# Another order for the first half of a hand-ordered attention and gated-MLP kernel

## The chip, the cores and the metric

The kernel runs on one core of a Trainium2 chip. The time is device time in microseconds; the span is the part of it that one profiled execution covers, from the first instruction's start to the last one's end. The core's engines work side by side, each through its own list of instructions in order: PE multiplies (PEld is its loading of weights), DVE, ACT and POOL work on tiles, and SP issues transfers between the chip's memory and the core's. Semaphores hold an instruction until what it needs is there.

## The reference

A retention layer without a softmax (8 batches, 8 heads, 576 positions, 64 numbers per head) makes x, and one gated MLP with a mixing over positions follows.

```python
scores = scale * np.matmul(q, k.transpose(0, 1, 3, 2))
Dmat = np.where(rel >= 0, gamma[:, None, None] ** rel[None, :, :], 0.0)
x = np.matmul(scores * Dmat, v)          # then heads side by side: (8, 576, 512)

h = gelu(x @ w_in)                       # w_in 512 x 1024, tanh form
u, v = (h[..., :512], h[..., 512:])
v_n = (v - mu) / np.sqrt(var + 1e-06) * g_ln
v_s = np.einsum('ts,bsd->btd', w_sg, v_n) + b_sg[None, :, None]
return (x + (u * v_s) @ w_out).astype(np.float32)
```

## The kernel before

**Tiling.** Two batches make a pair, and there are four pairs. A pair's 1152 rows are nine tiles of 128, so the output has 36 tiles, numbered 0 to 35. The attention is worked in blocks of one or two tiles, five per pair, so twenty blocks, 0 to 19 (of 2, 2, 1, 2 and 2 tiles). For a block, k, q and v are loaded (L457, or L460 in two halves for the one-tile blocks), scaled by powers of gamma and cast (L503; k at L493), q and k are turned by PE (L540) and copied out by DVE (L555), the scores (L591) are masked by DVE into `ret` (L604, L607), and the prefix product of k and v (L627) goes into a running sum (L652, L655), which lets a block do without the scores against all blocks ahead of it. The output (L673) is drained by ACT into `xT` (L730).

**The MLP.** Each tile of x is multiplied with the V half of w_in (L741); ACT applies the gelu (L748), DVE takes mean and variance (L756, L757), POOL the reciprocal root in four small operations (L761 to L764), and ACT writes the normalised tile (L776; L773 for the middle tile, which both batches of a pair share). The U half is multiplied at L788 and drained with a gelu at L798. When a batch's tiles are there, the mixing product with w_sg (L807) runs, DVE multiplies it with u (L817), and each output tile is a product with w_out and the addition of x (L833, L838). The first nine tiles are drained by ACT (L853), the later ones by DVE together with the addition of x (L855), for which SP turns x by a transfer (L847). SP stores each tile (L860).

**Things that happen once.** PE starts with "fillers", multiplications of zeros into a scratch tile that nothing reads (L357). The V half of w_in is loaded first (L381 into `xT`), the U half later (L381 into `uT`); DVE (L388) and ACT (L390) cast them. w_sg comes in three loads (L402 twice, L406), is cast by ACT into `wnat` (L413), turned by PE (L921) and copied by DVE (L925). The vectors g_ln and b_sg are turned by PE (L866) and worked into `col` by ten small DVE operations (L870 to L880), and PE turns them back into rows (L887, DVE L891). w_out is loaded into `uT` (L424).

**What sets the order.** Each of these steps is a job with a number, an engine, the jobs that it needs and the buffers that it takes. A string, `ORDER`, names the jobs in a row; a job's place among those of its own engine is its place in that engine's program, and `f10` in the string is a filler of ten units (two units make one multiplication of 128x256). The planner computes start times with its own costs only to bring the jobs of different engines into one sequence for the program; the order on each engine is that of the string. Buffers go round in rings (eight `ld`, three `vb`, four `ob`, two `pp` of PSUM), and a job that takes a buffer waits for the last reader of it. All loads, the turning transfers and all stores are issued by SP, one after another: an issue whose buffer is not free, or a store whose tile is not yet drained, holds what stands behind it.

Of the kernel before, what the change touches and what calls it, by code (L numbers as in the profile page):

```python
# [22 lines left out]
PR = dict(PB0=10000.0, O=4000.0, PB=9900.0, S=2000.0, S2=400.0, Z=1901.0, V=6000.0, V2=900.0, U=1260.0, W=4000.0, WS=19000.0, slack=60.0, pen=500.0)  # L23

ORDER = (
# [33 lines left out]
)  # L59


# [1144 lines left out]
```

## Time and profile before

| | |
|---|---|
| time, median of 3 runs | 214.62 us (214.43 to 214.93) |
| span of the profiled execution | 211.4 us |
| busy: PE, DVE, ACT, POOL | 197.6, 152.5, 116.8, 118.3 us |
| moved by transfers | 48.37 MB |

In the profile a row of a timeline gives the start and length of a group of instructions, its engine, line, operation and tiles, how many they are, and in brackets how long the engine stood idle before and what released it. The table by stretches gives busy times between two moments, the clock that PE was granted (1.00 is full), and the share of time in which the transfer engines had packets (it can pass 1, since packets overlap).

### The profile page before, as it was taken

Reading aid. Unit: us, or ns where it says so; the run is one execution under the profiler, and the core shown is the slowest. Engines: PE = TensorE matmul, PEld = TensorE weight load, DVE = VectorE, ACT = ScalarE, POOL = GpSimd, SP = SyncE. Lnnn points to the kernel's source line nnn. Section 1 sums busy time; section 2 is a strip of 40 time slices with the busy share of each in tenths; the row PEclk is TensorE's granted clock in tenths of the full one; section 3 lists DMA queues with packets and bytes.
Section 4 is the critical chain, followed back from the end, with each engine's and each line's share of the span. In section 5 each row is a group of like instructions: output and inputs, shape, how many; then the busy total and the mean of one; then the engine's idle time right before and its main releaser. Section 6 shows DMA issues by size and latency. Waiting matters only on the chain.

```text
span 211.4 us, 7911 instructions
## 1 busy us (share of the span) xinstructions
PE 197.6 (93%) x3384; PEld 137.8 (65%) x3416; DVE 152.5 (72%) x291; ACT 116.8 (55%) x207; POOL 118.3 (56%) x169
## 2 busy tenths in 40 slices
PE   7939999988999999999999999999999999999992
PEld 6727586666676677666767677566677675656661
DVE  3296498877888287967888875897865688576673
ACT  5230598892486954579585452776248349334400
POOL 8735158998667859993769679147582313022000
PEclk9985999999999999999999999999999999999999
DMA  6999999999899999999999999999999902586655
GB/s 164 335 276 305 170 374 295 231 291 340 192 248 296 296 324 276 214 328 189 243 285 109 243 307 206 198 323 182 222 172 148 270 0 78 149 153 174 176 172 198
DMA packets 85910, 48.37 MB, mean 229 GB/s; under 512 B 37035, under 2 KB 79283, under 8 KB 85875
## 3 DMA queue, kind: packets, MB, share of 16 engines
q1 hardware_dynamic: 85856, 47.87, 97.3%
q8 instruction: 26, 0.43, 0.9%
q14 instruction: 10, 0.07, 0.2%
q10 hardware_dynamic: 18, 0.00, 0.0%
HBM read 32.79 MB, written 9.44 MB: 200 GB/s over the span
## 4 chain that ended last, share of the span: by engine, by line
PE 79%; DVE 9%; issue 3%; POOL 3%; DMA 3%; ACT 1%; DVEq 0%; SPq 0%; POOLq 0%
PE wp L807 17%; PE hu L788 13%; PE op L838 13%; PE hv L741 12%; PE scr L357 6%; PE pp L673 6%; PE pp L591 4%; PE pp L540 3%; DMA ld<-in_v_dram 3%; DVE ret L604 2%; PE zp L627 2%; POOL vb L503 1%; DVE bst L756 1%; PE op L833 1%; POOL qb L503 1%
## 5 line engine op out<-in xcount | busy, mean ns | idle before, releaser
L807 PE MATMUL wp<-wT,vn 128*128 128x288 bf16 x256 | 41.1, 286 | 0.7 <-issue 0.6
L503 POOL TENSOR_TENSOR vb<-ld,gpow 128x1024 bf16<-128x1024 f32 (+1 forms) x20 | 34.5, 1731 | 11.6 <-DMA ld<-in_v_dram 8.8
L604 DVE TENSOR_TENSOR ret<-pp,msk 128x1024 bf16<-128x1024 f32 x32 | 38.3, 1215 | 3.4 <-PE pp L591 3.4
L788 PE MATMUL hu<-xT,w_in 128*128 128x256 bf16 (+1 forms) x320 | 36.8, 262 | 0.2
L817 DVE TENSOR_TENSOR uT<-wp,uT 128x288 bf16<-128x288 f32 x64 | 27.6, 451 | 12.4 <-PE wp L807 11.2
L741 PE MATMUL hv<-w_in,xT 128*128 128x512 bf16 x122 | 34.7, 380 | 1.7 <-ACT xT L730 0.3
L838 PE MATMUL op<-w_out,uT 128*128 128x512 bf16 (+1 forms) x138 | 34.4, 373 | 0.6 <-issue 0.2
L776 ACT ACTIVATE vn<-vg,mv 128x512 bf16<-128x512 f32 x32 | 25.3, 809 | 15.3 <-POOL mv L764 15.2
L748 ACT ACTIVATE vg<-hv 128x512 f32<-128x512 f32 x36 | 21.3, 596 | 21.8 <-PE hv L741 16.6
L788 PEld LDWEIGHTS <-w_in 128*128 128x128 bf16 x320 | 28.1, 98 | 7.2 <-issue 0.8
L756 DVE BATCH_NORM_STATS2 bst<-vg 128x6 f32<-128x512 f32 x36 | 24.7, 685 | 9.3 <-ACT vg L748 9.3
L730 ACT ACTIVATE xT<-pp 128x512 bf16<-128x512 f32 (+1 forms) x40 | 20.8, 550 | 18.1 <-PE pp L673 18.1
L807 PEld LDWEIGHTS <-vn 128*128 128x128 bf16 x256 | 24.4, 98 | 9.6 <-issue 0.7
L761 POOL TENSOR_SCALAR mv<-mv 128x2 f32<-128x2 f32 (+1 forms) x20 | 4.5, 224 | 44.7 <-DVE mv L757 37.8
L503 POOL TENSOR_TENSOR qb<-ldq,gpow 128x1024 bf16<-128x1024 f32 x14 | 26.9, 1934 | 4.0 <-DMA ldq<-in_q_dram 4.0
L798 ACT ACTIVATE uT<-hu 128x512 bf16<-128x512 f32 x36 | 21.2, 594 | 13.0 <-PE hu L788 12.9
L855 DVE TENSOR_TENSOR ob<-op,xr 128x512 f32<-128x512 f32 (+1 forms) x28 | 18.4, 669 | 8.3 <-PE op L838 6.3
L838 PEld LDWEIGHTS <-uT 128*128 128x128 bf16 x148 | 13.7, 98 | 11.3
L741 PEld LDWEIGHTS <-xT 128*128 128x128 bf16 x144 | 13.2, 98 | 12.0 <-ACT xT L730 0.2
L807 PE MATMUL wp<-wT,vmid 128*128 128x288 bf16 x64 | 18.0, 287 | 0.1
L357 PE MATMUL scr<-warm 128*128 128x256 f32 (+1 forms) x52 | 16.5, 489 | 1.2 <-DVE warm L316 1.2
L357 PEld LDWEIGHTS scr<-warm 128*128 128x128 f32 x52 | 13.0, 271 | 3.9 <-DVE warm L316 1.2
(100 smaller groups left out, 261.7 us busy)
## 6 DMA issues: line engine op xcount, KB each, us to landing
out_dram<-ob SPq DMA_DIRECT2D x35, 256.0 KB, 3.5
ld<-in_k_dram SPq DMA_DIRECT2D x16, 512.0 KB, 6.9
ld<-in_v_dram SPq DMA_DIRECT2D x16, 512.0 KB, 7.0
ldq<-in_q_dram SPq DMA_DIRECT2D x7, 1024.0 KB, 9.6
xT<-in_moe_w_sg_dram SPq DMA_DIRECT2D x2, 576.0 KB, 8.4
ld<-in_q_dram SPq DMA_DIRECT2D x2, 512.0 KB, 7.0
xT<-in_moe_w_in_dram SPq DMA_DIRECT2D x1, 1024.0 KB, 8.0
ld<-in_k_dram SPq DMA_DIRECT2D x8, 128.0 KB, 6.0
```

Source lines behind the costliest of these rows:

```text
L357: nc.tensor.matmul(scr[:, :w], warm[:, :128], warm[:, :w], start=True, stop=True, skip_group_check=True)
L503: ve.tensor_tensor(dst, src, g.unsqueeze(len(src.shape) - 1).to_broadcast(list(src.shape)), op=Alu.mult)
L604: ins = nc.vector.tensor_tensor(ret[:].rearrange("p r (k t) -> p (r k) t", k=2), sc[:].rearrange("p r (k t) -> p (r k) t", k=2), (msk2 if ...
L741: ins = nc.tensor.matmul(hv[:], xTs[p][:, m, kk, :], w_in[:, kk, F2:], start=(kk == 0), stop=(kk == KK - 1))
L748: unfence(nc.scalar.activation(vgs[i][:], cur.pop(("hv", i))[:], Act.Gelu_apprx_tanh), ("V", i))
L756: nc.vector.bn_stats(bst[:], vgs[i][:])
L776: nc.scalar.activation(vn[:], vg[:], Act.Identity, scale=mv[:, s, 2:3], bias=mv[:, s, 3:4])
L788: ins = nc.tensor.matmul(hu[:, n, :], w_in[:, kk, 128 * c:128 * c + 128], xTs[p][:, m:m + w, kk, :], start=(kk == 0), stop=(kk == KK - 1), ...
L798: unfence(nc.scalar.activation(uTs[p][:, c0:c1, 128 * m:128 * m + 128 * w], cur.pop(("hu", i, half))[:], Act.Gelu_apprx_tanh), ("U", i, half))
L807: ins = nc.tensor.matmul(ps[:], vns[t0 + j][e][:, 128 * c:128 * c + 128], wT[e][j][:, half * HS:(half + 1) * HS], start=(j == 0), stop=(j ...
L817: ins = nc.vector.tensor_tensor(uTs[p][:, c, col:col + HS], cur.pop(("wp", b, c, half))[:], uTs[p][:, c, col:col + HS], op=Alu.mult)
L838: ins = nc.tensor.matmul(op[:], uTs[p][:, c, r], w_out[:, c, cs], start=(p >= XP and c == 0), stop=(c == KK - 1), skip_group_check=True)
```

## The change

Only `ORDER` changes. The same jobs stand in it, and the tiles and buffers are the same. On PE the two programs agree from the V product of tile 17 on, on DVE and ACT and POOL from about the same place, and on SP from the turning transfer of tile 11. Ahead of that the order differs on each engine. The fillers go from eight of 47 units in all (1, 3, 5, 10, 2, 3, 14 and 9, in another sequence) to ten of 52 units (10, 2, 3, 12, 6, 4, 8, 2, 4 and 1). The string takes 31 lines instead of 39, so all later line numbers are 8 smaller in the changed kernel (L457 is L449 there, L860 is L852).

```diff
 ORDER = (
-    '1 f3 0 f1 2 f5 f10 3 73 6 f2 75 17 f3 76 103 7 104 72 105 106 77 107 8 78 271 201 4 5 199 f14 272 200 273 16 13 '
-    '108 202 22 274 15 79 276 12 109 277 278 14 111 279 280 275 110 112 283 281 80 21 23 282 205 293 20 203 294 f9 '
...
+    '1 0 6 2 73 8 f10 75 74 103 104 7 76 f2 f3 106 108 3 9 72 105 23 107 f12 199 271 200 201 273 109 202 110 f6 111 272 276 112 277 278 293 274 203 5 4 294 '
+    '279 204 16 f4 280 12 205 281 283 206 295 17 275 13 284 296 297 282 11 298 15 285 299 300 10 290 f8 286 301 118 291 292 f2 304 14 287 24 305 307 21 113 '
...
```

The start of DVE's program, behind the powers of gamma. Before, q of block 0 (`qb`) stands behind the work on the columns:

```order
L870 COPY col<-tp 128x9
L872 TENSOR_SCALAR colt<-col 128x4
L873 SCALAR_TENSOR_TENSOR colt<-col,colt 128x4
...
L880 TENSOR_TENSOR col_76<-colr,col_76 128x10
L503 TENSOR_TENSOR qb<-ld,gpow 128x2x8x64
L894 MEMSET wnat 128x5x32
```

And in the change:

```order
L495 TENSOR_TENSOR qb<-ld,gpow 128x2x8x64
L862 COPY col<-tp 128x9
L864 TENSOR_SCALAR colt<-col 128x4
L865 SCALAR_TENSOR_TENSOR colt<-col,colt 128x4
...
L872 TENSOR_TENSOR col_76<-colr,col_76 128x10
L886 MEMSET wnat 128x5x32
```

The preparation of q has moved ahead of the ten operations, which follow it in their old order.

The start of SP's program, the loads (`xT` is the V half of w_in, `uT` its U half). Before:

```order
L457 DMA ld<-in_k_dram 128x8x128
L457 DMA ld<-in_q_dram 128x8x128
L457 DMA ld<-in_v_dram 128x8x128
L381 DMA xT<-in_moe_w_in_dram 128x4x512
L457 DMA ld<-in_q_dram 128x8x128
L406 DMA ld<-in_moe_w_sg_dram 64x576
L457 DMA ld<-in_k_dram 128x8x128
L457 DMA ld<-in_v_dram 128x8x128
L402 DMA xT<-in_moe_w_sg_dram 128x2x576
L460 DMA ld<-in_k_dram 64x8x64 x2
```

And in the change:

```order
L449 DMA ld<-in_k_dram 128x8x128
L449 DMA ld<-in_q_dram 128x8x128 x2
L449 DMA ld<-in_v_dram 128x8x128 x2
L449 DMA ld<-in_k_dram 128x8x128
L373 DMA xT<-in_moe_w_in_dram 128x4x512
L373 DMA uT<-in_moe_w_in_dram 128x4x512
L449 DMA ldq<-in_q_dram 128x8x256
L394 DMA xT<-in_moe_w_sg_dram 128x2x576
L452 DMA ld<-in_q_dram 64x8x64 x2
L398 DMA ld<-in_moe_w_sg_dram 64x576
```

All of q, k and v of blocks 0 and 1 now stand ahead of w_in, and its U half, which was the eleventh load behind the V half, follows it at once, ahead of w_sg.

SP's program around the store of output tile 6 (`ob_2405` before, `ob_2216` in the change), with the buffers' numbers. Before:

```order
L460 DMA ld_2045<-in_q_dram 64x8x64 x2
L457 DMA ld_2146<-in_k_dram 128x8x128
L457 DMA ldq_2191<-in_q_dram 128x8x256
...
L460 DMA ld_2656<-in_k_dram 64x8x64 x2
L457 DMA ld_2713<-in_k_dram 128x8x128
L860 DMA out_0_dram<-ob_2405 128x512
L457 DMA ld_2734<-in_v_dram 128x8x128
```

And in the change:

```order
L452 DMA ld_1801<-in_q_dram 64x8x64 x2
L449 DMA ld_2018<-in_v_dram 128x8x128
L449 DMA ld_2066<-in_v_dram 128x8x128
L852 DMA out_0_dram<-ob_2216 128x512
L449 DMA ld_2351<-in_k_dram 128x8x128
L852 DMA out_0_dram<-ob_2085 128x512
L449 DMA ld_2375<-in_k_dram 128x8x128
L452 DMA ld_2380<-in_k_dram 64x8x64 x2
```

Thirteen transfers that stood ahead of tile 6's store stand behind it now, k of block 13 (`ld_2351`) the first of them. On ACT, tile 7 (`ob_2228` there) is now drained directly ahead of tile 6, and on PE the two tiles' products stand side by side, 6 ahead of 7.

54 rows, old and new, of the table ORDER are left out of this document.

## The prediction

> **What bounds the kernel now.** I read the page's busy shares and its chain first.
>
> ```profile
> PE 197.6 (93%) x3384; PEld 137.8 (65%) x3416; DVE 152.5 (72%) x291; ACT 116.8 (55%) x207; POOL 118.3 (56%) x169
> PE 79%; DVE 9%; issue 3%; POOL 3%; DMA 3%; ACT 1%; DVEq 0%; SPq 0%; POOLq 0%
> ```
>
> PE bounds the whole, so time is to be had only where PE idles or multiplies fillers. The table by stretches says where (columns: stretch, its length, busy us of PE, PEld, DVE, ACT, POOL, granted clock, DMA share, GB/s).
>
> ```profile
> 10.00:15.00 5.00, 1.47 (x69) 1.05 (x68) 4.66 (x14) 1.72 (x3) 2.14 (x2) 0.91 1.17 284
> 15.00:20.00 5.00, 4.74 (x41) 3.85 (x42) 4.14 (x7) 0.28 (x1) 3.50 (x3) 0.50 1.18 296
> 25.00:45.00 20.00, 19.28 (x443) 14.15 (x443) 17.67 (x34) 17.86 (x32) 15.74 (x23) 1.00 1.09 289
> 135.00:170.00 35.00, 34.28 (x594) 23.91 (x590) 26.74 (x52) 19.98 (x36) 17.69 (x24) 1.00 1.05 213
> 170.00:208.00 38.00, 37.41 (x370) 24.04 (x371) 26.88 (x52) 15.96 (x26) 5.32 (x16) 1.00 0.52 136
> ```
>
> Only the start has slack to win: PE works 1.47 of 5 us, then at half clock. From 135 us on it idles 0.72 + 0.59 = 1.3 us in 73, so what is late at 135 us stays late. The PE timeline shows the start and the first product with w_sg (46.92, L807).
>
> ```profile
> 13.17 0.41 PE L540 MATMUL pp<-ident,qb 64*128 64x64 bf16 x16 [2.82 <-DVE qb L503]
> 15.26 1.07 PE L591 MATMUL pp<-qT 64*64 64x128 bf16 x32 [0.97 <-DVE qT L555]
> 16.25 5.58 PE L357 MATMUL scr<-warm 128*128 128x256 f32 x14
> 24.19 1.67 PE L741 MATMUL hv<-w_in,xT 128*128 128x512 bf16 x7 [0.34 <-ACT xT L730]
> 26.62 2.21 PE L357 MATMUL scr<-warm 128*128 128x256 f32 x10
> 45.81 0.31 PE L673 MATMUL pp<-qT,zb 64*64 64x128 bf16 x8 [0.70 <-DVE ret L604]
> 46.92 0.66 PE L807 MATMUL wp<-wT,vn 128*128 128x288 bf16 x4
> ```
>
> **The start, part by part.** The first transpose (13.17) waits for block 0's q on DVE, which stands behind ten small operations on the columns of g_ln and b_sg:
>
> ```profile
> 9.20 0.17 DVE L870 COPY col<-tp 128x9 f32<-128x9 f32 x1 [5.68 <-PE tp L866]
> 11.89 1.23 DVE L503 TENSOR_TENSOR qb<-ld,gpow 128x1024 bf16<-128x1024 f32 x1
> 16.45 2.36 DVE L604 TENSOR_TENSOR ret<-pp,msk 128x1024 bf16<-128x1024 f32 x2
> ld<-in_q_dram SPq DMA_DIRECT2D x1, 512.0 KB, 5.5
> ld<-in_v_dram SPq DMA_DIRECT2D x1, 512.0 KB, 6.7
> xT<-in_moe_w_in_dram SPq DMA_DIRECT2D x1, 1024.0 KB, 8.0
> 25.04 0.60 ACT L748 ACTIVATE vg<-hv 128x512 f32<-128x512 f32 x1 [0.34 <-PE hv L741]
> ```
>
> The three load rows are from the DMA view, cut to SP's issues at 1.29, 1.91 and 3.29 us: q landed at 6.8, v at 8.6, the V half of w_in at 11.3. In the change q's preparation goes first, 6.9 to 8.1; the columns follow (11.89 - 9.20 = 2.7), to 10.8, then the zeroing of wnat (0.9) and the copy of the transposes (1.2), to 12.9. The first scores start near 13.0, not 15.26: **2.2 us earlier**. The filler of 14 held PE to 21.8, though its scores were masked by 16.45 + 2.36 = 18.8: 3 us more, so in all up to about 5 at the first output. Two loads limit this. The w_in halves now follow six loads of 512 KB, against three; at 1.8 us each (8.6 - 6.8), then 2.7 for 1 MB (11.3 - 8.6), the V half lands at 6.8 + 4 x 1.8 + 2.7 = 16.7, is cast in about 1 us, and the V product starts at 19 to 20, not 24.19. So **4 to 5 us of lead** there, before the fillers. Their sum grows from 47 units to 52; a unit is 2.21 / 10 = 0.22 us at full clock: 1.1 us, but most of it stands in waits.
>
> How much reaches 46.92? The product waits for ACT's last norm of the first half. ACT's string from the first gelu at 25.04 takes 21.9 us, and the 25 to 45 row shows it and DVE at 88 to 89%: the work is spread over a longer time, hardly reduced. Two pieces of it, 1.0 us, now stand behind. From a first gelu at 20.3 that gives 41.2 at the least; the U half of w_in comes sooner, but the second half of w_sg now stands behind 7.2 MB, not 5.0, and at 289 GB/s lands 29 to 31 us in, with its casts, turns and copies to come. I add 1 to 2 for it: 42 to 43.5, a lead of 3.4 to 4.9. Of that, 1.1 us (45.81 to 46.92, block 3's output) is only work put behind, and that block's score and prefix product some 0.3 more. Net lead: 2.0 to 3.5, taken as **2.5 us**; the bounds are 0 (the load and the full engines eat it all) and 4.9.
>
> Costed at nothing: POOL's zeroing of w_sg's tiles, moved up into POOL's idle time ahead of block 2's preparation (1.1 us if that cover is gone), and PE's "issue" time, 3% of the chain or 6.3 us, since PE's program is the same but for two filler multiplications; its pauses can fall elsewhere, and the range holds a quarter of them, 1.5 us to either side.
>
> **The SP queue.** SP issues in order; a store holds all loads behind it. In the change tile 6's store stands ahead of thirteen transfers that were ahead of it, k of block 13 first. Up to it SP issues 22.27 MB (loads and four stores). In the kernel before, exactly 22.27 MB were issued by the end of this first row:
>
> ```profile
> 81.22 2.41 SPq L460 DMA_DIRECT2D ld<-in_q_dram  x2
> 84.14 0.40 SPq L457 DMA_DIRECT2D ld<-in_k_dram  x1
> ```
>
> So, the stream being as full (DMA share 1.09 from 25 to 45 us, and nearly all nines in the last row below), SP is there near 83.6. When is tile 6 done? The PE rows:
>
> ```profile
> 87.71 0.64 PE L540 MATMUL pp<-ident,qb 64*128 64x64 bf16 x32
> 88.28 1.04 PE L741 MATMUL hv<-w_in,xT 128*128 128x512 bf16 x3
> 89.25 0.37 PE L627 MATMUL zp<-vb,kb 64*64 64x64 bf16 x12
> 90.78 0.40 PE L833 MATMUL op<-ident,xT 128*128 128x128 bf16 x4
> 91.88 0.39 PE L833 MATMUL op<-ident,xT 128*128 128x128 bf16 x4
> 92.96 0.39 PE L833 MATMUL op<-ident,xT 128*128 128x128 bf16 x4
> 93.80 1.08 ACT L853 ACTIVATE ob<-op 128x512 f32<-128x512 f32 x2
> ```
>
> Tile 6 starts at 91.88. The change puts tile 7 (1.08, as tile 6 took to 92.96), a transpose (87.71 to 88.28: 0.57) and a run of block 8 to 10 work (89.25 to 90.78: 1.53) behind it, 3.2 us: 88.7. But ACT drains tile 7 ahead of tile 6, so both products (2 x 1.08) and two drains (1.08) go by: the store is free at 88.7 + 2.2 + 1.1 = 92.0 at the old pace, 89.5 with the lead of 2.5. SP stands 83.6 to 89.5. A load that meets an empty queue takes 4.2 us (block 0's k), one in a full queue 5.5 (issue at 84.14):
>
> ```profile
> ld<-in_k_dram SPq DMA_DIRECT2D x1, 512.0 KB, 4.2
> ld<-in_k_dram SPq DMA_DIRECT2D x1, 512.0 KB, 5.5
> DMA  9989999999999994959999999995989996999999
> ```
>
> So k of block 13 lands near 89.9 + 4.2 = 94.1; the load in the same place of the stream landed at 84.14 + 5.5 = 89.6: the loads run **4.5 us late**. The last row is the DMA share of 83 to 127 us in 40 slices of 1.1 us: idle that a late stream can fill is about 20 tenths of a slice, 2.2 us. At the k load of block 16, by when both orders have issued the same 31 MB, **2.3 us** are left. Bounds: nothing, if queued bytes cover the stop; 4.6, if nothing is made up.
>
> Who waits for that k? POOL, ACT and PE in turn:
>
> ```profile
> 127.04 1.04 POOL L493 CAST kb<-ld 128x1024 bf16<-128x1024 f32 x1 [1.62 <-DMA ld<-in_k_dram]
> 128.59 1.90 POOL L503 TENSOR_TENSOR vb<-ld,gpow 128x1024 bf16<-128x1024 f32 x1
> 130.58 0.23 POOL L761 TENSOR_SCALAR mv<-mv 128x2 f32<-128x2 f32 x1
> 132.24 0.81 ACT L776 ACTIVATE vn<-vg,mv 128x512 bf16<-128x512 f32 x1 [1.76 <-POOL mv L764]
> 133.65 1.08 ACT L730 ACTIVATE xT<-pp 128x512 bf16<-128x512 f32 x2
> 134.78 0.68 PE L591 MATMUL pp<-qT,kT 64*64 64x128 bf16 x32
> ```
>
> POOL waits 1.62 us for the load; behind it, in POOL's order, stand block 14's v and the reciprocal roots; ACT's norm waits 1.76 for those, and drains block 13's output (133.65 to 134.73) only then; that frees the buffer into which PE writes block 14's scores at 134.78. The room is 0.05 us, and the order here is the old one in both kernels. So the 2.3 us pass through whole, whatever PE had gained by then: it waits. After it 1.3 us of idle can give back little; I take 0.1. **Sum: +2.2 us** on a span of 211.4; the median of the runs shown is 214.62, 3.2 above that span, so 216.8.
>
> [...] The 0.50 of 15 to 20 us came after 5 us with 1.47 of PE work. In the change no PE gap of the start is worked out above 1.5 us. [...]
>
> **Rivals.**
> - **The lead survives.** If the queued loads cover SP's stop, or SP reaches it later, k of block 16 is not late, and PE keeps 2.5, or 1.5 to 4: 212.1 (210.6 to 213.1). For it: stores stand at SP anyhow; against: 5.9 us of stop are more than the 5.5 that a load spends in a full queue. 0.24.
> - **PE is throttled again.** Short work with gaps between 13 and 21 us, as in the row 10 to 15; 4 us of work at half clock lose about 2. The lead is 0.5, tile 6 is free 2 us later, the loads run 2 later: 218.8. 0.12.
> - **The mid stretch eats the lead.** DVE and ACT at 88% give back 1.5 of it: the store is free at 91, k of block 16 is 3.8 late: 218.3. It decides once SP stops over 7 us. 0.13.
> - **No difference.** Loads late by just what nobody waits for, and the lead lost to masks and norms: 214.6. 0.06.
>
> **How the numbers follow.** The forecast, 216.8 (215.1 to 217.9), has 0.45. It is slower, as are throttle and mid stretch: 0.45 + 0.12 + 0.13 = 0.70; faster 0.24; within 0.2% (0.43 us, about what a measurement of this kernel can tell from no change) 0.06. The range reaches down to 212.6, which leaves out about 0.12 of the lead's case, and up to 220.4, where a lag of 4.6 meets a throttled start, which leaves out some 0.05.
>
> **What would show it.** Right: first scores near 13 us, first V product at 19 to 20, first product with w_sg before 44; a long stop of SP ahead of a store at 80 to 91 us with a hole in the DMA row behind it; POOL's wait for block 16's k, and a PE wait at block 14's scores of 2 us or more. Wrong: SP issues that store at once, or no PE wait near 135 us; then the lead stands at the end. A granted clock of 0.5 to 0.7 in 13 to 21 us would show the throttle.

## The result, and the profile after

The changed kernel takes 222.69 us (median of 4 runs, 222.11 to 225.37) against 214.62: a ratio of 1.0415, 95% interval 1.0335 to 1.0495. It is slower, as forecast, but by 8.1 us and not 2.2, and it lies above the stated range. The profiled execution spans 220.8 us against 211.4. Run to run, one kernel scatters by up to 4% on some of the chips used (the kernel before took 210.87 to 219.08 us on one, and one run of e10 took 482.7), so the ratios below, each of the fast runs alone against the kernel before on the same chip, say more than the medians.

The table by stretches of the changed kernel, in the columns shown before the result:

```profile
10.00:15.00 5.00, 1.28 (x6) 0.77 (x5) 4.73 (x11) 0.00 (x0) 3.64 (x4) 1.00 1.16 321
15.00:20.00 5.00, 4.66 (x110) 3.50 (x114) 2.99 (x5) 0.38 (x1) 1.87 (x2) 0.66 1.06 379
20.00:25.00 5.00, 4.23 (x114) 2.74 (x112) 4.04 (x6) 2.74 (x5) 0.00 (x0) 1.00 0.58 182
25.00:45.00 20.00, 18.78 (x321) 13.96 (x321) 13.27 (x28) 17.67 (x32) 13.41 (x20) 1.00 1.09 277
145.00:180.00 35.00, 34.12 (x552) 23.59 (x557) 26.13 (x51) 19.13 (x35) 17.69 (x24) 1.00 1.04 211
180.00:217.00 37.00, 36.69 (x364) 23.45 (x365) 25.88 (x50) 15.70 (x26) 5.32 (x16) 1.00 0.52 137
```

Between 10 and 15 us PE still works only 1.28 of 5 us and is again at a reduced clock behind it (0.66), and from 20 to 25 the transfers fall to a share of 0.58. From 145 us on PE idles as little as in the kernel before (1.2 us in 72). So the loss lies ahead of 145. The PE timeline shows the places:

```profile
15.35 0.42 PE L583 MATMUL pp<-qT 64*64 64x128 bf16 x16 [4.07 <-DVE qT L547]
23.23 1.03 PE L733 MATMUL hv<-w_in,xT 128*128 128x512 bf16 x3
46.85 0.65 PE L799 MATMUL wp<-wT,vn 128*128 128x288 bf16 x4
...
65.16 0.58 PE L583 MATMUL pp<-qT,kT 64*64 64x128 bf16 x25 [1.70 <-issue]
109.70 0.21 PE L583 MATMUL pp<-qT,kT 64*64 64x128 bf16 x1 [1.95 <-issue]
128.27 0.28 PE L799 MATMUL wp<-wT,vmid 128*128 128x288 bf16 x1 [1.14 <-ACT vg L740]
143.67 0.64 PE L583 MATMUL pp<-qT,kT 64*64 64x128 bf16 x32 [2.45 <-ACT xT L722]
```

The first scores (15.35) gained nothing against 15.26, the first V product 1 us, the first product with w_sg nothing (46.85 against 46.92), and block 14's scores start at 143.67, 8.9 us later than before. "Issue" in the brackets stands for a pause to which the profile shows no cause. SP's timeline shows what that last place waited for:

```profile
11.08 0.77 SPq L449 DMA_DIRECT2D ldq<-in_q_dram  x1
22.61 0.37 SPq L394 DMA_DIRECT2D xT<-in_moe_w_sg_dram  x1
...
80.84 2.11 SPq L449 DMA_DIRECT2D ld<-in_v_dram  x2
93.90 0.36 SPq L852 DMA_DIRECT2D out_dram<-ob  x1
94.35 0.40 SPq L449 DMA_DIRECT2D ld<-in_k_dram  x1
...
128.04 1.44 SPq L449 DMA_DIRECT2D ld<-in_k_dram  x1
```

POOL's timeline has the cast of that last load, block 16's k:

```profile
136.38 1.04 POOL L485 CAST kb<-ld 128x1024 bf16<-128x1024 f32 x1 [4.39 <-DMA ld<-in_k_dram]
```

And the transfer view's share for 83 to 127 us, in slices of 1.1 us:

```profile
DMA  5996000000387999988999995992763799999999
```

SP stands 10.8 us, from 11.85 to 22.61, ahead of the load of w_sg, and 10.9, from 82.95 to 93.90, ahead of tile 6's store. During the second stop the transfers run dry for six slices. Block 16's k is cast at 136.38, 9.3 us later than before.

### The profile page after: what moved, and what is told of

Same layout as the page of the kernel before. It is cut to its first block, busy times and chain, and to the rows that moved or that the text cites. A ratio compares the mean times of both kernels' runs of the same rounds, so it can differ in the third digit from the quotient of the medians.

```text
span 220.8 us, 7911 instructions
## 1 busy us (share of the span) xinstructions
PE 199.0 (90%) x3388; PEld 136.9 (62%) x3418; DVE 154.3 (70%) x291; ACT 116.3 (53%) x207; POOL 117.8 (53%) x169
## 5 line engine op out<-in xcount | busy, mean ns | idle before, releaser
L748 DVE BATCH_NORM_STATS2 bst<-vg 128x6 f32<-128x512 f32 x36 | 24.6, 684 | 13.7 <-ACT vg L740 13.7
L790 ACT ACTIVATE uT<-hu 128x512 bf16<-128x512 f32 x36 | 21.1, 594 | 13.6 <-PE hu L780 13.5
L733 PEld LDWEIGHTS <-xT 128*128 128x128 bf16 x144 | 13.2, 98 | 12.8 <-ACT xT L722 0.5
L830 PEld LDWEIGHTS <-uT 128*128 128x128 bf16 x148 | 13.7, 98 | 11.3
L349 PE MATMUL scr<-warm 128*128 128x256 f32 (+1 forms) x54 | 17.1, 464 | 1.9 <-DVE warm L308 1.2
L583 PE MATMUL pp<-qT,kT 64*64 64x128 bf16 x448 | 11.7, 219 | 6.2 <-issue 3.6
```

The source lines that it names most:

```text
L733: ins = nc.tensor.matmul(hv[:], xTs[p][:, m, kk, :], w_in[:, kk, F2:], start=(kk == 0), stop=(kk == KK - 1))
L748: nc.vector.bn_stats(bst[:], vgs[i][:])
L790: unfence(nc.scalar.activation(uTs[p][:, c0:c1, 128 * m:128 * m + 128 * w], cur.pop(("hu", i, half))[:], Act.Gelu_apprx_tanh), ("U", i, half))
L830: ins = nc.tensor.matmul(op[:], uTs[p][:, c, r], w_out[:, c, cs], start=(p >= XP and c == 0), stop=(c == KK - 1), skip_group_check=True)
```

## The experiments

All twelve edit only the order string, unless said otherwise. Each diff gives the edit as the rows of the engine it concerns, with the tile or block behind the row.

**Tile 6's store, taken back out of the loads' way.**

```diff
 SP: v of blocks 10 and 11
-store of tile 6
 k of block 13, store of tile 4, k of blocks 14 and 12
-store of tile 7
 q of block 13, k of block 15, v of blocks 15 and 13
+store of tile 6
+store of tile 7
```

> The changed kernel with only SP's order edited: the stores of tiles 6 and 7 go behind v of block 13. Theory A (SP's stop of 10.9 us at tile 6's store makes k of block 16 9.3 us late, and that k sets PE's block 14 scores): no stop of SP over 3 us between 80 and 100 us, POOL's cast of that k near 128 to 130 instead of 136.4, no PE wait at block 14's scores, and PE keeps only the 5.1 us by which it is late at the V product of tile 17, so 222.7 - 9.3 + 5.1 = 218.5 (217.3 to 219.7). Rival B (the stop only uncovers what PE had lost already): 221.5 or more. Rival C (the late loads also caused PE's own 5.1): under 217.

Measured: 216.71 us, ratio 1.0118 (1.0057 to 1.0179). One row each of SP's, POOL's and PE's timelines of this kernel:

```profile
83.27 0.78 SPq L449 DMA_DIRECT2D ld<-in_k_dram  x1
```

```profile
128.38 1.04 POOL L485 CAST kb<-ld 128x1024 bf16<-128x1024 f32 x1
```

```profile
137.79 0.68 PE L583 MATMUL pp<-qT,kT 64*64 64x128 bf16 x32
```

Block 13's k goes out at 83.27, block 16's is cast at 128.38 without a wait, and PE goes into block 14's scores without one. SP still stands 4.0 us, from 92.93 to 96.89, where none over 3 was expected. Two moved stores give back 6.0 of the 8.1 us by the medians, 0.030 of 0.0415 by the ratios, more than theory A's sum: what I had put down to PE is smaller here too (rival C's direction, and by the median its number). The wait of 1.14 at 128.27 is gone, and the pauses sum to 1.3 us, not 4.9; whether the late loads had caused the pauses is not shown.

**The same store, moved into the loads' way in the kernel before.**

```diff
 SP: both q loads of block 12
+store of tile 6
 k of block 14
 ...
-store of tile 6
```

> The kernel before with only SP's order edited: tile 6's store goes up behind the two q loads of block 12, the place by bytes that it has in the changed kernel. Theory A: SP stops from 83.6 to about 97 (ACT drains the tile at 96.1 to 96.7), k of block 16 comes 10 to 13 us later, PE waits for it at block 14's scores, and nothing is made up afterwards: 224 to 227. Rival B (queued bytes and slack cover the stop): 214.6 to 216.

Measured: 222.38 us, 1.0328 (1.0268 to 1.0387). SP's rows, then PE's:

```profile
81.21 2.28 SPq L460 DMA_DIRECT2D ld<-in_q_dram  x2
97.23 0.34 SPq L860 DMA_DIRECT2D out_dram<-ob  x1
...
128.05 2.22 SPq L457 DMA_DIRECT2D ld<-in_k_dram  x1
```

```profile
110.16 0.64 PE L627 MATMUL zp<-vb,kb 64*64 64x64 bf16 x32 [3.92 <-POOL vb L503]
114.13 0.26 PE L627 MATMUL zp<-vb,qb 64*64 64x64 bf16 x3 [1.84 <-POOL vb L503]
144.71 0.68 PE L591 MATMUL pp<-qT,kT 64*64 64x128 bf16 x32
```

One store in another place, and the kernel before is nearly as slow as the changed one. The stop is 13.7 us long, as worked out. The loss is 7.7 us by the medians (214.67 before on that chip) and 0.033 by the ratio, below theory A's 9 to 12. PE does not pay it at block 14's scores, which start without a wait, but earlier, at the prefix products of blocks 11 and 12, whose v comes late. Behind the first of these waits the granted clock is 0.50 from 110 to 115 us and 0.63 from 115 to 120, so that the two waits cost more than their 5.8 us.

**The casts of w_in's V half first.** SP's second stop, at 11.85, is one that I had not seen: the load of w_sg writes the staging tile of the V half, so it waits for that half's casts, and ACT's cast stands behind the drain of block 0.

```profile
21.05 0.60 ACT L722 ACTIVATE xT<-pp 128x512 bf16<-128x512 f32 x1 [4.56 <-PE pp L665]
21.54 1.05 ACT L382 ACTIVATE w_in<-xT 128x1024 bf16<-128x1024 f32 x1
```

(ACT's timeline of the changed kernel.)

```diff
 ACT: first sum of block 0
+cast of w_in, V half
 drain of block 0 (first tile)
-cast of w_in, V half
 DVE: copy of block 0's sum
+cast of w_in, V half
 copy of block 1's transposes, ...
-cast of w_in, V half
```

> The changed kernel with the casts of w_in's V half put ahead of block 0's drain on ACT and ahead of block 1's copy of transposes on DVE. SP's load of w_sg writes the same staging tile and waits for these casts. Theory D: that load is issued near 19 instead of 22.6 and the hole of the DMA row at 20 to 25 us shrinks by some 3 us; the end hardly moves, since tile 6's store stops SP again: 221 to 222.7. Rival E (the hole at 12 to 22 us is what makes all loads late): 219 or less.

Measured: 222.67 us, 1.0347 (1.0303 to 1.0391). SP issues the load of w_sg at 17.80 instead of 22.61, and the time is the same within the noise: theory D. With tile 6's store in its place the earlier loads bring nothing that can be told.

**POOL's v ahead of q.**

```diff
 POOL: zeroing
-q of block 1
 v of block 0
+q of block 1
```

> The changed kernel with POOL preparing v of block 0 ahead of q of block 1, so that POOL has nothing to do from 8.8 to about 10.4 us while DVE works on the columns. Theory F (DVE's small operations wait for POOL's running operation to end): no operation on the columns takes over 0.7 us before 10.4, the column work ends by 11.5 instead of 13.2, and block 0's first scores start at 13.0 to 13.8 instead of 15.35; the end 221 to 222.7. Rival G (these operations are slow by themselves): two of them still take 1.7 us and the scores start at 15.3.

Measured: 220.37 us, 1.0237 (1.0157 to 1.0317). DVE's rows of the changed kernel and POOL's beside them:

```profile
8.14 0.65 DVE L864 TENSOR_SCALAR colt<-col 128x4 f32<-128x4 f32 x1
9.02 1.75 DVE L866 SCALAR_TENSOR_TENSOR colr<-colt,col 128x4 f32<-128x4 f32 x1
10.81 0.18 DVE L867 RECIPROCAL colr<-colr 128x4 f32<-128x4 f32 x1
10.90 1.74 DVE L868 COPY colr<-col 128x5 f32<-128x5 f32 x1
```

```profile
8.19 0.57 POOL L892 MEMSET wT<- 64x576 bf16 x1
8.85 1.91 POOL L495 TENSOR_TENSOR qb<-ld,gpow 128x1024 bf16<-128x1024 f32 x1
10.72 1.89 POOL L495 TENSOR_TENSOR vb<-ld,gpow 128x1024 bf16<-128x1024 f32 x1
```

The same two operations in this kernel on DVE, then POOL's first operation behind the zeroing, and PE's first scores:

```profile
9.02 0.16 DVE L866 SCALAR_TENSOR_TENSOR colr<-colt,col 128x4 f32<-128x4 f32 x1
9.31 0.14 DVE L868 COPY colr<-col 128x5 f32<-128x5 f32 x1
```

```profile
10.56 1.90 POOL L495 TENSOR_TENSOR vb<-ld,gpow 128x1024 bf16<-128x1024 f32 x1 [1.80 <-DMA ld<-in_v_dram]
```

```profile
12.22 0.42 PE L583 MATMUL pp<-qT 64*64 64x128 bf16 x16 [0.89 <-DVE qT L547]
```

Each long operation on DVE ends where POOL's running one ends: 9.02 + 1.75 = 10.77 with 8.85 + 1.91 = 10.76, and 12.64 with 12.61. With POOL idle the same two take 0.16 and 0.14, and the first scores start 3.1 us earlier. Theory F holds, and the time falls below the 221 that it gave. The reciprocal between them did not wait: it started at 10.81, beside POOL's operation from 10.72 to 12.61, and took 0.18 us. No run here told the forms apart further.

**Both edits that gained, then all three.** No new edits; e5 takes those of e1 and e4, e6 those of e3 as well.

> The changed kernel with both edits that gained: the stores of tiles 6 and 7 behind v of block 13 on SP, and v of block 0 ahead of q of block 1 on POOL. If the two losses are separate (a stop of SP, and DVE waiting for POOL at the start), the gains add: 216.7 - 2.3 = 214.4 (213.4 to 215.4), level with the kernel before. If the start's 3 us are taken back by DVE and ACT in the middle, as the forecast's third rival has it: 216 to 217.

> The kernel of the run above with the casts of the V half of w_in ahead of block 0's drain on ACT and block 1's copy on DVE as well, so that SP's load of w_sg goes out near 17.8. With SP's stop at tile 6 gone, 1 to 4 us of earlier loads can count now: 213.2 (212.2 to 214.4). If the loads of the first 45 us are not what the engines wait for: the same as the run above within 0.5.

Measured: 215.44 us, 1.0114 (1.0059 to 1.0168), and 216.32 us, 1.0141 (1.0047 to 1.0236). By the ratios the gain of e4 does not add to that of e1 (1.0118): the forecast of adding up missed, and e6 is no better. The profiled execution of e5, its fastest of twelve, spans 210.8 us and has its first product with w_sg at 44.06, so the start's lead is there in that one. The other eleven took 214.3 us or more. The granted clock was 1.000 in the profiled one and 0.973 to 0.997 in those. In e4's profiled execution, at 0.992, it is 0.66 from 20 to 25 us, and the product comes at 45.31. So the clock can take a part of the lead; what takes the rest was not seen.

**Parts of the change alone, in the kernel before.** DVE's q ahead of the columns (e7); the filler of 14 cut to 4 (e8); the U half of w_in directly behind the V half on SP (e12); and e8 with e7 (e11).

```diff
 e7, e11: DVE
+q of block 0
 ten operations on the columns
-q of block 0
 e8, e11: PE
-f14
+f4
 e12: SP
 V half of w_in
+U half of w_in
 ...
-U half of w_in
```

> The kernel before with one part of the change alone: on DVE q of block 0 ahead of the work on the columns. POOL's preparation of v runs from 8.75 to 10.65 in both, so the column work still ends near 11.9; the copy of the transposes starts near 12.8 instead of 13.98 and the first scores near 14 instead of 15.26. The filler of 14 behind them then ends 1.2 earlier: 213.6 (212.8 to 214.4). If the masks, norms and loads behind set the pace: 214.6 within 0.4.

> The kernel before with one part alone: the filler of 14 units behind the first scores cut to 4. PE is free for block 0's output near 18.9 (its masks end at 18.8) instead of 21.8. If that filler held the start: the V product starts 2 to 3 us earlier and the end gains 0.5 to 2: 213.4 (212.5 to 214.2). If the loads of w_sg and of the U half of w_in set the pace up to 36 us, as their waits before suggest: 214.6 within 0.5.

> The kernel before with two parts: the filler of 14 cut to 4, and on DVE q of block 0 ahead of the work on the columns. First scores near 14, block 0's output near 17.5 and the first V product near 20. If the start's lead passes through as in e8 (2.6 us there): 1 more, 210.5 (209.5 to 211.5). If w_sg's and the U half's loads then set the pace: 211.5 as in e8.

> The kernel before with one part alone: SP loads the U half of w_in directly behind the V half. All loads up to block 2's v come 2.7 us later and nothing needs the U half before 36 us. w_sg's last rows land near 27 instead of 24.5, its casts and turns start 1 to 3 us later than 28.7: 216.5 (215.5 to 218). If those turns had slack: 214.6 within 0.7.

Measured: e7 213.97 us, 1.0017 (0.9964 to 1.0071); e8 211.46, 0.9889 (0.9808 to 0.9971); e11 213.29, 1.0011 (0.9971 to 1.0050); e12 215.51, 1.0074 (1.0022 to 1.0125). PE's rows of e8 (two), then of e12 (two):

```profile
21.41 1.67 PE L741 MATMUL hv<-w_in,xT 128*128 128x512 bf16 x7 [0.34 <-ACT xT L730]
44.62 0.66 PE L807 MATMUL wp<-wT,vn 128*128 128x288 bf16 x4
```

```profile
28.98 0.23 PE L921 MATMUL wtp<-ident,wnat 128*128 128x128 bf16 x1 [1.38 <-ACT wnat L413]
29.56 1.51 PE L921 MATMUL wtp<-ident,wnat 128*128 128x128 bf16 x24 [0.34 <-ACT wnat L413]
```

In e8 the V product starts 2.8 us earlier and the first product with w_sg 2.3: that filler did hold the start, and the lead survives there. It is the only kernel here that beats both, by 1.1% (0.3 to 1.9%, from six runs). With q first as well (e11) the gain is gone; why is open. In e12 the turns of w_sg wait for ACT's cast, as worked out: the U half's place costs 0.2 to 1.2%. e7 alone gives nothing that can be told from none, though its first product with w_sg comes at 45.45.

**Where the blocks of PE's program begin.** A filler function that adds small multiplications behind the first filler:

```diff
 def fill(n, cold):
 ...
+            for _ in range(28 if cold else 0):
+                nc.tensor.matmul(scr[:16, :16], ident[:, :16], ident[:, :16], start=True, stop=True, skip_group_check=True)
```

(28 on top of e5's order; 88 in e10, on top of e8's, where they replace the filler of 10.)

> The kernel of e5_later_and_swap (the changed kernel with the two edits that gained) with 28 small multiplications of 16x16 behind the first filler, 56 instructions that move where the blocks of 256 in which PE's program is fetched begin. Theory H (PE stands, as issue, where a block of its program is worked off before the next is there, some 5 us): with this shift the worst blocks hold 3.0 instead of 3.8 us of work, and the issue waits grow from 2.3 to 5 or 7 us; 218 to 221. Rival I (issue waits are chance, wherever the blocks begin): 215.4 within 1.5 and the same waits.

> The kernel of e8_short_filler (the kernel before with the filler of 14 cut to 4) with the filler of 10 replaced by 88 small multiplications of 16x16, which move the blocks by some 150 instructions, where no block holds under 4.7 us of work (3.4 in e8). Theory H: issue waits fall from 1.2 to under 0.7 us, the end gains 0.5 to 1.5: 210.4 (209.4 to 211.4). Rival I: 211.5 within 1.

Measured: e9 219.20 us, 1.0254 (1.0216 to 1.0291); e10 213.46, 0.9969 (0.9933 to 1.0005). The waits of PE by what ended them (us in total, times, the longest): e5, then e9.

```profile
PE zp L619 <- issue: 1.3, 1, 1.3
PE hv L733 <- issue: 0.5, 3, 0.2
PE pp L583 <- issue: 0.3, 1, 0.3
PE op L830 <- issue: 0.2, 1, 0.2
```

```profile
PE hv L735 <- issue: 2.9, 4, 2.4
PE pp L534 <- issue: 2.2, 2, 1.3
PE wp L801 <- issue: 1.3, 1, 1.3
PE op L832 <- issue: 0.2, 1, 0.2
```

With the program shifted by 56 instructions these waits sum to 6.6 us, not 2.3, and the time is 1.4 points longer, as theory H had it. In e10 they were to fall below 0.7 us and rose from e8's 1.2 to 3.4 (1.45, 0.88 and 0.60 the longest), and the first product with w_sg comes at 46.14, not 44.62: that forecast missed, and the 5 us for a block's arrival, my estimate, which no run here measures, are too rough to choose a shift by.

Where the pauses stand can be counted. Taking PE's multiplications and weight loads of a trace in order as records, every such pause of 0.25 us or more in the fourteen profiled executions stands 157 to 188 records behind a multiple of 256, (some records are missing from a trace), whatever the instruction: at record 1973 in the changed kernel (scores, 65.16) and in e9 (transposes, 60.48). The profile also counts 26 packets of 16 KB in one instruction queue, about one for every 256 of PE's 6800 records. So the places are those of theory H. The sizes do not follow from the places: the change, e1, e3, e4, e5 and e6 have the same PE program, and their pauses sum to 4.9, 1.3, 4.0, 3.2, 2.3 and 4.8 us, at different ones of these places. So how much of e9's rise is due to the shift is open; its time is clear of e5's.

## Why the prediction was wrong

**The mechanism was right.** Tile 6's store stopped SP; block 16's k came late; POOL, ACT and PE waited in turn (4.39, then 2.45 us at block 14's scores); and nothing was made up after it (8.9 us late at 143.67, 9.4 at the end of the span). e1 shows it in the changed kernel; e2 shows in the one before that such a stop costs PE about as much, there by way of other loads. SP's arrival by bytes, 83.6, was met at 82.95.

**The size failed at three terms of the sum.**

1. "The store is free at ... 89.5 with the lead of 2.5." It was free at 93.90. There was no lead: at 92.0 "at the old pace" the step would have been 1.9 us short instead of 4.4. PE's row is the start of the two tiles' products, ACT's their drain:

```profile
90.42 0.39 PE L825 MATMUL op<-ident,xT 128*128 128x128 bf16 x4
```

```profile
92.79 1.09 ACT L845 ACTIVATE ob<-op 128x512 f32<-128x512 f32 x2 [1.28 <-PE op L830]
```

PE came to them at 90.42, not 88.7. Up to there its pauses sum to 2.3 us (21.80 and 65.16), against 0.9 in the kernel before, which is of the size of that lateness.
2. "The columns follow (11.89 - 9.20 = 2.7), to 10.8." They took 5.3 us, 7.94 to 13.2. The 2.7 was read where POOL ran for only part of the time, and even there one operation on four columns had taken 1.28 us beside POOL's v (8.75 to 10.65):

```profile
9.40 1.28 DVE L872 TENSOR_SCALAR colt<-col 128x4 f32<-128x4 f32 x1
```

The change moves POOL's q of block 1 beside them. This is the missing lead of the scores: 15.35, not 13.0, and with POOL idle 12.22 (e4); and it is that of the first product with w_sg, which e5's profiled execution, with the same edit, has 2.9 us ahead of the kernel before. "Cast in about 1 us" failed too: the half landed near 16.7, as worked out (11.85 and SP's wait of 4.8 us for it), but the cast was behind a drain on ACT, and SP's load of w_sg behind the cast. That second stop was missed, though e3 shows no cost of it here: with the casts first the V product starts at 23.31, and the time is the same.
3. "Idle that a late stream can fill is ... 2.2 us." Block 13's k went out 10.2 us later than the load in its place (94.35 against 84.14), block 16's k 9.9 later than before, when its row was this:

```profile
118.18 3.05 SPq L457 DMA_DIRECT2D ld<-in_k_dram  x1
```

So 0.35 us was made up. In e2 more was: 13.5 late at the first load (97.67 against 84.14) and 9.9 at block 16's k (128.05). So how much a stream recovers is not read off its idle slices.

With the measured end of the stop the forecast's own chain gives the loss: block 13's k at 94.35 + 4.2 = 98.6, against 89.6, is 8.9 us late, and with nothing made up that is 214.6 + 8.9 = 223.5, against 222.7 measured. The 3.2 us between the span and the time was not a constant either: behind the change it is 1.9 (222.69 against 220.8), so that the spans differ by 9.4 us and the medians by 8.1.

**The pauses** ("issue") were costed at nothing with 1.5 us to either side; by the table of PE's waits, which lists fewer of them than the chain, they grew from 1.4 to 4.9 us in the profiled executions. How much of the 8.1 us is theirs is open: in e1, with the same PE program, they sum to 1.3. The longest, 1.95 us at 109.70, stands ahead of the wait for block 16's k, and by the forecast's own chain cost nothing.

**The rivals.** "The lead survives" did not come; "throttled again" came in part (0.66 from 15 to 20 us), behind 4.07 us of waiting; "the mid stretch eats the lead" had nothing to eat. The prediction's sum has the full clock at the start, with no gap of PE above 1.5 us; that such gaps leave it full, no row of the kernel before had shown. In the kernel before a gap of 2.82 us (to 13.17) stands ahead of the 0.50 of 15 to 20 us, in the changed one the gap of 4.07 ahead of its 0.66. But e4 has 0.66 from 20 to 25 us with no wait of PE over 1.25 us ahead of it, and in e5's profiled execution, with the same order at the start and a wait of 1.34 us ahead of 19.00, the clock stayed at 1.00, so the waits alone do not decide it.

**The account.** Of 1.0415, the place of two stores is 0.030 (1.0415 - 1.0118). What is left, 0.012 (0.006 to 0.018), was not traced to a part: the U half's place alone costs 0.007 in the kernel before (0.002 to 0.012), and the pauses, 1.3 us in e1, are no longer there than in the kernel before.

## What to carry to other kernels

A store in a queue of loads is a wait, of 10.9 us here and 13.7 in e2. Its length is the time from SP's arrival there, which the bytes issued so far told to 0.7 us here, to the drain of its tile, counted on PE's late side as well as on its early one; a load without slack then passes most of it on (8.9 of 10.2 us here). Before moving small DVE operations, look at what POOL runs beside them, since a row of 0.16 us can become one of 1.75. And a filler that runs beyond what it covers is cheap to cut and worth a try: e8 gained 1.1%, though e10 and e11, with the same cut and one thing more, gained nothing that can be told.

## What was not expected of the hardware

DVE operations on four and five numbers per partition took 1.75 and 1.74 us beside POOL's, to the end of its instruction, and 0.16 and 0.14 without. PE's pauses without a cause, up to 2.40 us long in e9, stand 157 to 188 records behind multiples of 256 in the count of its instructions, and which of these places has one changed between executions of the same PE program. And a stop of SP of 13.7 us in one order cost 7.7 us, one of 10.9 in the other 6.0: neither was hidden, though the 16 transfer engines had shown shares of 0.9 and more on both sides of it.
